# Pooled attention and two feed-forward blocks: in the first batch every second part of the attention weights meets the values in plain float32

## The chip, the cores and the metric

The program runs on one core of a Trainium2 chip. The metric is the device time of one execution, in microseconds (us); the number to compare with is the median of three runs of the kernel before, 1444.92 us (1443.05 to 1446.12). Engines: PE multiplies matrices (PEld is its weight load), ACT, DVE and POOL do elementwise work, SP issues most DMAs. PE's results go to PSUM, the tile `banks` of the program; the other tiles lie in SBUF.

## What is computed

```python
q_pool = q.reshape(B, H, S // 2, 2, D).mean(axis=3)            # B=4, H=8, S=1152, D=64
scores = (q_pool @ k.transpose(0, 1, 3, 2)) / np.sqrt(D)
attn = np.exp(scores - scores.max(-1, keepdims=True))
attn = attn / (attn.sum(-1, keepdims=True) + 1e-9)
x = attn @ v                                                   # then heads side by side: 2304 x 512
g = s * np.maximum(x @ w_in, 0.0) ** 2 + b                     # 512 -> 2048
x = g @ w_out                                                  # 2048 -> 512
out = (1 / (1 + np.exp(-(x @ w_gate)))) * (x @ w_val) @ w_out2 # 512 -> 1536 -> 512
```

All of it is float32. To keep float32's accuracy at a fast matmul, most operands are split in two: a rounded high part in the type `fp32r` and a low part, the rest.

## The kernel before, in words

**Planner.** The code does not issue instructions directly. Each step is added to a plan with a name, the engines that may do it, what it reads and writes and a rank; `Plan.order` then writes one order per engine, picking at each moment the ready step of the lowest rank for a free engine. A step with two engines goes to whichever is free first. A table, `MOVED`, shifts the rank and the place of every step by its name. Buffers are slots of a fixed number (`ROOM`); a slot's next tenant waits for the last one's readers. The order on every engine is therefore fixed in the program, and each engine runs its rows strictly in that order.

**Stages.** Attention goes batch by batch and in pairs of heads (`pair_prep` loads q, k and v of a pair and makes their transposed and split forms). Batch 0 is done by query rows (`pair_rows`), the other batches by key columns (`half_head_sums`). After a batch the first feed-forward block follows (`ffn1`) while the next batch's attention goes on beside it, and at the end the second block (`ffn2`) takes two batches at once. So the stretch up to about 191 us is batch 0's attention alone, with a few loads and splits of weights (the `w` steps) and a little of batch 1 in between.

**Batch 0's attention.** `block` multiplies the transposed q by k (L901), takes the row maximum on DVE (L908, L911) and the exponential with its sum on ACT (L915). `group(j, g, blocks, mid)` then turns the weights round: for one head `j` and a set of query blocks it goes over the 9 key chunks, two chunks at a time, or one at a time where the group also holds the middle block `mid`. Such a step is called a unit here. A unit's transposes (L946, and for the middle block a plain float32 matmul with the identity, L948) put 512 or 256 weights a partition into a bank (320 with the middle block). There are 4 head pairs, and in each pair two groups of 5 units and two of 9, so 28 units a pair and 112 in all.

From the bank a unit goes one of two ways, in turn (`unit[0] % 2`). On the *copy path* ACT copies the bank to an SBUF tile (`r p`, L469 `pp<-banks`), ACT or POOL makes the high part (`r p hi`, L462 or L464, `g<-pp`) and POOL or DVE the low part (`r p lo`, L472). On the *direct path* ACT rounds the bank into the high part (`r pT hi`, L469 `g<-banks`) and DVE subtracts it from the bank (`r pT lo`, L475). Either way PE then multiplies each chunk twice, high and low part, by the split values `vt` (L968, step `r pv`):

```python
for w in range(2):
    for i, c in enumerate(cs):
        nc.tensor.matmul(acc.t[:, :n], lhsT=vt[j].t[:, c, :2 * D], rhs=part(t, w)[:, i * n:(i + 1) * n],
                         start=(c == 0 and w == 0), stop=(c == NK - 1 and w == 1))
```

`vt` holds the low part of v in its first 64 columns and the high part in the next 64, so `acc` has two halves, which a copy and an addition put together at the group's end (`r o`, `r x add`). At a pair's end `x` is divided by the sums (L987 to L1004).

The values come by a load into one raw tile (`v load`, L683, `vn`, one slot), from which `v hi` and `v lo` make `vt` (two slots); the raw tile is free again as soon as `v lo` has read it.

Of the kernel before, what the change touches and what calls it, by code (L numbers as in the profile page):

```python
# [23 lines left out]

ROOM = dict(
    w=4, raw=3, xy=2, xx=1, r=2, g=4,
    qn=1, kn=1, vn=1, qT=2, kT=2, vt=2, st=6, pp=6,
    sg=2, mx=2, mc=2, r9=1, x=1, s=2, rs=1, rr=1,
    yy=1, yl=1, h=4, fo=9,
    ps=4, pr=8, pm=1, acc=5, ff=6, p2=3, wd=2, bank=8,  # L30
# [5 lines left out]


MOVED = {
    "q load": (-1, -9),
    "k load": (0, -100),  # L40
    "v load": (2.5, -102),
    "v hi": (0, 97),
    "v lo": (18, 38),
    "q add": (-3, 29),
    "q twice": (-2.5, -30),
    "pr qT": (-1.5, 69),
    "pr q hi False": (-6.5, 100),
    "pr q lo False": (-11, 68),
    "pr q hi True": (-6, 3),
    "pr q lo True": (45.5, -33),  # L50
    "pr kT": (-19.5, 79),
    "pr k hi": (-39.5, 10),
    "pr k lo": (-40, -29),
    "s b load": (-6.5, -46),
    "r qk 1": (-0.5, -351),
    "r max": (0, 32),
    "r - max": (-40, 11),
    "r exp": (40.5, -80),
    "r pT": (-32.5, 21),
    "r p": (-40, 84),  # L60
    "r p hi": (21.5, -68),
    "r p lo": (0, -21),
    "r pv": (-34, -88),
    "r pT hi": (-40, 101),
    "r pT lo": (8.5, 12),
    "r o": (0, 49),
    "r x add": (3, 116),
    "r qk 2": (-40, 112),
    "r sums": (60, 108),
    "r sums eps": (0, 33),  # L70
    "r 1 / sums": (-2, 2),
    "r spread": (8, -150),
    "r rows": (-0.5, -245),
    "r rows mid": (2, 74),
    "r x / sums": (55.5, -57),
    "r x / sums mid": (3, 63),
    "r end": (16, -111),
    "ps qT": (3, -59),
    "ps q hi False": (53, 89),
    "ps q lo False": (-27.5, -110),  # L80
    "ps kT": (-11, -1),
    "ps k hi": (11.5, -104),
    "ps k lo": (-37, 59),
    "xx hi": (59.5, -1),
    "xx lo": (60, 37),
    "w load": (-18, 34),
    "w top": (-19, 94),
    "w scale": (-13.5, -136),
    "w low": (-31, 18),
    "w join": (38.5, 14),  # L90
    "w sign": (-40, -93),
    "w hi": (-40, -95),
    "w lo": (-25.5, -32),
    "w keep": (0, -20),
    "one": (-33, -6),
    "ff xx up": (60, 125),
    "ff relu": (-11, -3),
    "square": (-40, 114),
    "g hi": (7, 20),
    "g lo": (-16, 108),  # L100
    "ff down": (55, -143),
    "ff y": (-11, 66),
    "column sum": (-7.5, 111),
    "ff y add": (31.5, 21),
    "bias": (-27, 149),
    "y bias": (-19, -30),
    "y store": (-25.5, 72),
    "qk": (0, 17),
    "s copy": (15.5, -5),
    "s max": (-14, 27),  # L110
    "max T": (-9.5, -130),
    "max": (46, -9),
    "max rows": (-27.5, -98),
    "s - max": (38.5, 169),
    "exp": (4, -43),
    "p hi": (-23, -97),
    "p lo": (-10.5, 18),
    "pv hi": (-40, 73),
    "pv lo": (18.5, -4),
    "sums": (36, -116),  # L120
    "x": (27.5, -8),
    "sums out": (6, -15),
    "sums in": (4, 112),
    "1 / sums spread": (0, -90),
    "1 / sums out": (0, -25),
    "1 / sums in": (3, 31),
    "x / sums": (26.5, -166),
    "1 / sums": (8, 22),
    "w fetch": (-3.5, -5),
    "w come": (59, -37),  # L130
    "x store": (42.5, -95),
    "turn": (42, -63),
    "yy load": (43.5, 45),
    "yy hi": (0, 79),
    "yy lo": (0, -86),
    "p2 yy up": (0, 47),
    "gate": (0, -40),
    "gate val": (-40, -79),
    "h hi": (19.5, -93),
    "h lo": (0.5, 95),  # L140
    "down 2": (-25.5, 139),
    "out": (60, 118),
    "out add": (-40, -64),
    "out store": (0, 82),
    "xx load": (42, -28),
    "p2 xx up": (-7, -54),
    "p2 relu": (13, 19),
    "p2 down": (0, -20),
    "p2 y": (19.5, -12),
    "p2 y add": (8, -91),  # L150
}


# [193 lines left out]
def kernel(  # L347
# [93 lines left out]
    def mm(n):  # L441
        return max(n / 2.4, 45) + 13.5
# [223 lines left out]
    def pair_prep(b, hp):  # L666
# [13 lines left out]
        for j in range(2):  # L680
            src = v[b, h0 + j].rearrange("(p c) d -> p c d", c=NK)
            vn = slot("ld", "vn", [P, NK, D])
            dma("v load", P * NK * D * 4, lambda vn=vn, src=src: nc.sync.dma_start(out=vn.t, in_=src), [], [vn], AT)  # L683
            t = plan.slot("vt", lambda k: vts[k])
            copy_sb("v hi", NK * D, lambda t=t: t.t[:, :, D:2 * D], lambda vn=vn: vn.t, [vn], [(t, 0)], AT)
            tt_sb("v lo", NK * D, lambda t=t: t.t[:, :, :D], lambda vn=vn: vn.t, lambda t=t: t.t[:, :, D:2 * D].bitcast(F32),
                  ALU.subtract, [vn, (t, 0)], [(t, 1)], AT)
            vt.append(t)

        def pairs_of_q():  # L690
# [188 lines left out]
    def pair_rows(hp, prep, x):  # L879
# [50 lines left out]
        unit = [0]  # L930

        def group(j, g, blocks, mid):

            n = 256 + (64 if mid else 0)
            acc = bank("acc")
            step = 1 if mid else 2
            for c0 in range(0, NK, step):
                cs = list(range(c0, min(NK, c0 + step)))
                ps = bank("pr")
                t = g_slot()  # L940
                m = n * len(cs)

                def issue(cs=cs, ps=ps):
# [19 lines left out]
                unit[0] += 1  # L963

                def pv(cs=cs, t=t):
                    for w in range(2):
# [180 lines left out]
```

## Time and profile before

| what | value |
| --- | --- |
| median of 3 runs | 1444.92 us (1443.05 to 1446.12) |
| the profiled execution: its time, its span | 1447.07 us, 1445.3 us |
| PE busy, weight load busy | 1380.4 us (96%), 1310.8 us (91%) |
| DVE, ACT, POOL busy | 1041.4 us (72%), 929.2 us (64%), 736.6 us (51%) |
| batch 0's attention | 0 to about 191 us |

The profiled execution took 2.15 us more than the median of the runs; 1.8 us of its time lies outside the span. "Busy" counts an instruction from start to end, and on PE the ends of one instruction overlap the start of the next. "Idle before" an instruction is time its engine waited, with the instruction that ended the wait behind the arrow. A wait costs time only where something that sets the end hangs on it.

### The profile page before, as it was taken

How to read it: one execution, taken by the hardware profiler on the slowest of the kernel's cores; microseconds unless marked ns; L12 is line 12 of the kernel's file. 1: busy time of each engine (PE TensorE's matmuls, PEld its weight loads, DVE VectorE, ACT ScalarE, POOL GpSimd, SP SyncE). 2: the span in 40 equal slices, each digit the busy share in tenths (PEclk: the TensorE clock that was granted, in tenths of full speed). 3: DMA queues.
4: the chain of work that ended last, by engine and by line, in shares of the span. 5: the costliest groups of instructions: out<-in, count | busy, mean ns of one | idle time of the engine just before them, and what ended most of it. 6: DMA issues, size and time to landing. Idle time of an engine off the chain costs nothing.

```text
span 1445.3 us, 25059 instructions
## 1 busy us (share of the span) xinstructions
PE 1380.4 (96%) x9164; PEld 1310.8 (91%) x9164; DVE 1041.4 (72%) x1786; ACT 929.2 (64%) x1987; POOL 736.6 (51%) x675
## 2 busy tenths in 40 slices
PE   6988998999999999999999999999999899999998
PEld 6867888888989999999899999999998899989897
DVE  6889897899989889889988757557473127737552
ACT  6889887988889898988899645333232434434130
POOL 3577675888867466666765446233232004325130
PEclk9999999999999999999999999999999999999999
DMA  3156123446435142413331463122137444313112
GB/s 91 50 166 202 26 92 100 153 152 222 143 108 167 50 142 79 137 47 115 106 133 47 178 256 126 59 88 88 59 92 247 165 154 147 116 58 118 42 61 66
DMA packets 103044, 167.89 MB, mean 116 GB/s; under 512 B 44652, under 2 KB 80264, under 8 KB 93832
## 3 DMA queue, kind: packets, MB, share of 16 engines
q1 hardware_dynamic: 96008, 115.95, 26.1%
q0 software_dynamic: 6912, 50.33, 9.8%
q8 instruction: 72, 1.18, 0.3%
q14 instruction: 52, 0.43, 0.1%
HBM read 139.99 MB, written 26.28 MB: 115 GB/s over the span
## 4 chain that ended last, share of the span: by engine, by line
PE 62%; ACT 13%; DVE 9%; DMA 7%; issue 5%; POOL 4%; SPq 0%; DVEq 0%; ACTq 0%; POOLq 0%
PE banks L540 13%; PE banks L542 13%; PE banks L541 13%; PE banks L770 3%; PE banks L1050 3%; PE banks L1049 3%; PE banks L1048 3%; ACT st L796 3%; ACT st L469 3%; DVE mx L475 3%; DMA raw<-in_moe_w_in_dram 2%; PE banks L818 2%; ACT pp L462 2%; PE banks L819 2%; PE banks L823 2%
## 5 line engine op out<-in xcount | busy, mean ns | idle before, releaser
L472 POOL TENSOR_TENSOR pp<-st,pp 128x864 fp32r<-128x864 f32 x94 | 199.3, 2130 | 32.3 <-ACT pp L462 29.7
L542 PE MATMUL banks<-yy,w 128*128 128x384 f32 x576 | 192.8, 335 | 0.0
L541 PE MATMUL banks<-yy,w 128*128 128x384 f32 x576 | 192.8, 335 | 0.0
L540 PE MATMUL banks<-yy,w 128*128 128x384 f32 x576 | 192.7, 335 | 0.0
L469 ACT COPY st<-banks 128x288 f32<-128x288 f32 x432 | 150.2, 409 | 41.2 <-PE banks L770 35.5
L475 DVE TENSOR_TENSOR mx<-banks,mx 128x288 f32<-128x288 f32 x336 | 151.3, 451 | 21.0 <-ACT st L469 10.5
L770 PE MATMUL banks<-qT,kT 128*128 128x288 f32 x864 | 162.3, 304 | 1.9 <-DVE mx L475 1.0
L540 PE MATMUL banks<-xx,w 128*128 128x288 f32 x512 | 155.1, 303 | 8.2 <-DMA w<-d_1u_1u 5.7
L541 PE MATMUL banks<-xx,w 128*128 128x288 f32 x512 | 151.7, 296 | 0.0
L475 DVE TENSOR_TENSOR st<-st,banks 128x864 f32<-128x864 f32 x144 | 149.4, 1041 | 3.1 <-PE banks L748 3.0
L542 PE MATMUL banks<-xx,w 128*128 128x288 f32 x512 | 151.6, 296 | 0.0
L540 PE MATMUL banks<-g,w 128*128 128x288 f32 x448 | 136.7, 305 | 3.7 <-ACT xy L642 2.9
L796 ACT ACTIVATE st<-st 128x864 f32<-128x864 f32 x144 | 132.9, 931 | 11.1 <-DVE st L475 10.1
L497 POOL TENSOR_SCALAR raw<-raw 128x512 f32<-128x512 f32 x98 | 66.5, 679 | 138.2 <-DMA raw<-in_moe_w_val_dram 50.5
L541 PE MATMUL banks<-g,w 128*128 128x288 f32 x448 | 133.7, 298 | 0.0
L542 PE MATMUL banks<-g,w 128*128 128x288 f32 x448 | 133.5, 298 | 0.0
L770 PEld LDWEIGHTS banks<-qT,kT 128*128 128x128 f32 x864 | 126.4, 188 | 5.9 <-DVE mx L475 3.8
L500 ACT ACTIVATE raw<-raw 128x512 f32<-128x512 f32 x104 | 70.7, 683 | 94.6 <-POOL raw L497 88.1
L818 PE MATMUL banks<-pp,vt 128*128 128x288 f32 x432 | 121.9, 302 | 7.6 <-ACT pp L462 5.8
L819 PE MATMUL banks<-pp,vt 128*64 128x288 f32 x432 | 118.5, 295 | 0.0
L540 PEld LDWEIGHTS banks<-yy,w 128*128 128x128 f32 x576 | 108.1, 188 | 0.3
L541 PEld LDWEIGHTS banks<-yy,w 128*128 128x128 f32 x576 | 108.1, 188 | 0.3
(145 smaller groups left out, 3867.3 us busy)
## 6 DMA issues: line engine op xcount, KB each, us to landing
w<-d_1u_1u POOLq DMA_DIRECT2D x24, 1024.0 KB, 5.6
w<-d_1d_1d POOLq DMA_DIRECT2D x24, 1024.0 KB, 5.8
raw<-in_moe_w_out_dram SPq DMA_DIRECT2D x40, 512.0 KB, 3.6
raw<-in_moe_w_gate_dram SPq DMA_DIRECT2D x24, 512.0 KB
raw<-in_moe_w_val_dram SPq DMA_DIRECT2D x24, 512.0 KB, 4.2
qn<-in_q_dram SPq DMA_DIRECT2D x16, 576.0 KB, 4.2
kn<-in_k_dram SPq DMA_DIRECT2D x32, 288.0 KB, 4.0
vn<-in_v_dram SPq DMA_DIRECT2D x32, 288.0 KB, 2.7
```

The costliest lines, as they stand in the source:

```text
L469: act(name, n, lambda: nc.scalar.copy(out=out(), in_=in_()), r, w, rank, sbuf=False)
L472: shared(name, n, lambda e: ENGINE[e].tensor_tensor(out=out(), in0=in0(), in1=in1(), op=op), r, w, rank, 2.15)
L475: dve(name, n, lambda: nc.vector.tensor_tensor(out=out(), in0=in0(), in1=in1(), op=op), r, w, rank)
L497: shared("w top", 512, lambda e: ENGINE[e].tensor_scalar(out=words(1).bitcast(F32), in0=words(1).bitcast(F32), scalar1=F64_TOP, scalar2=-F ...
L500: act("w scale", 512, lambda: nc.scalar.mul(words(1).bitcast(F32), words(1).bitcast(F32), 2.0 ** -112), [], [top], rank)
L540: nc.tensor.matmul(ps(), lhsT=whi(), rhs=xhi(), start=first, stop=False)
L541: nc.tensor.matmul((ps_lo or ps)(), lhsT=whi(), rhs=xlo(), start=False, stop=False)
L542: nc.tensor.matmul(ps(), lhsT=wlo(), rhs=xhi(), start=False, stop=last)
L770: nc.tensor.matmul(ps.t[:, :HQ], lhsT=kT.t[:, c], rhs=qq[:, w, hf * HQ:(hf + 1) * HQ], start=(w == 0), stop=(w == 1))
L796: act("exp", 3 * HQ, lambda s=s: nc.scalar.activation(out=s.t, in_=s.t, func=AF.Exp), [], parts, AT)
L818: nc.tensor.matmul(acc.t[:, :HQ], lhsT=vt.t[:, 3 * i + c, D:], rhs=hi.t[:, c], start=(i == c == 0), stop=False)
L819: nc.tensor.matmul(acc.t[:D, :HQ], lhsT=vt.t[:, 3 * i + c, :D], rhs=hi.t[:, c], start=False, stop=False)
```

## The change

In `group`, the flag `unit[0]` is gone and a flag `split` starts every group as true. A unit with `split` takes the copy path as before. The unit after it is taken whole: one copy of the bank to an SBUF tile in float32 (`r pT whole`, on ACT or DVE, whichever is free), no high and low part, and one matmul a chunk in plain float32 by the raw values (`r pv whole`, L972 in the changed file), added to the lower half of `acc`. Then `split` is true again. The direct path is gone. The raw values of a head must now stay until their last whole matmul, so `vn` has two slots. All ranks of `MOVED` are other numbers.

```diff
-    qn=1, kn=1, vn=1, qT=2, kT=2, vt=2, st=6, pp=6,
+    qn=1, kn=1, vn=2, qT=2, kT=2, vt=2, st=6, pp=6,
...
-    "r pT": (-32.5, 21),
+    "r pT": (-37.5, -107),
...
+            t.whole = vn
             vt.append(t)
...
+            split = True
             for c0 in range(0, NK, step):
...
-                t = g_slot()
+                t = g_slot() if split else slot("pp", "pp", [P, 3 * HQ])
...
-                if unit[0] % 2 == 0:
+                if split:
                     pc = slot("pp", "pp", [P, 3 * HQ])
...
                 else:
-                    copy_ps("r pT hi", m, lambda t=t, m=m: part(t, 0)[:, :m], lambda ps=ps, m=m: ps.t[:, :m], [ps], [(t, 0)], AT)
-                    tt_dve("r pT lo", m, lambda t=t, m=m: part(t, 1)[:, :m], lambda ps=ps, m=m: ps.t[:, :m],
-                           lambda t=t, m=m: part(t, 0)[:, :m].bitcast(F32), ALU.subtract, [ps, (t, 0)], [(t, 1)], AT)
-                unit[0] += 1
+                    def whole(e, ps=ps, t=t, m=m):
+                        if e == "ACT":
+                            nc.scalar.copy(out=t.t[:, :m], in_=ps.t[:, :m])
+                        else:
+                            nc.vector.tensor_copy(out=t.t[:, :m], in_=ps.t[:, :m])
+
+                    plan.add("r pT whole", {"ACT": 50 + 0.833 * m, "DVE": 70 + 1.04 * m}, 0, whole, [ps], [t], AT)
+                    v32 = vt[j].whole
+
+                    def pv32(cs=cs, t=t, v32=v32):
+                        for i, c in enumerate(cs):
+                            nc.tensor.matmul(acc.t[:D, :n], lhsT=v32.t[:, c], rhs=t.t[:, i * n:(i + 1) * n],
+                                             start=False, stop=False)
+
+                    pe("r pv whole", len(cs) * (n / 0.6 + 25), pv32, [t, v32], [acc], AT)
+                    split = True
+                    continue
...
+                split = False
```

Per pair this makes 16 split and 12 whole units out of 14 and 14. In all, 48 units are whole (16 of 512 and 32 of 320 elements) and 64 chunks go by a float32 matmul (32 of 256 and 32 of 320 columns); 160 fast matmuls stay in L968's place out of 288. The line numbers of the changed file are one higher from L687 on and up to fifteen higher below `group`.

The order moves in many places. Three carry the prediction. First PE, in the first pair's group with the middle block (`g` tiles are split units, `pp` tiles whole ones, `st` the weights that are turned, `vn` and `vt` the raw and the split values). Before:

```order
L901 MATMUL banks<-kT_198,qT_176 128x384 x4
L968 MATMUL banks<-g_384,vt_117 128x320 x2
L968 MATMUL banks<-g_388,vt_117 128x320 x2
L946 MATMUL banks<-ident,st_235 128x128
L946 MATMUL banks<-ident,st_268 128x128
L948 MATMUL banks<-ident,st_275 128x64
```

Now:

```order
L902 MATMUL banks<-kT_200,qT_176 128x384 x4
L947 MATMUL banks<-ident,st_340 128x128
L947 MATMUL banks<-ident,st_382 128x128
L949 MATMUL banks<-ident,st_276 128x64
L902 MATMUL banks<-kT_200,qT_176 128x384 x2
L972 MATMUL banks<-pp_410,vn_182 64x320
L982 MATMUL banks<-g_376,vt_117 128x320 x2
```

Two units gave four fast matmuls; two units now give one float32 matmul (64 output partitions) and two fast ones, and transposes for a later unit stand ahead of them.

Second DVE at the same place, first before and then now:

```order
L475 TENSOR_TENSOR xy_427<-pp_417 64x256
L475 TENSOR_TENSOR g_388<-banks,g_388 128x320
L475 TENSOR_TENSOR g_430<-banks,g_430 128x320
L908 TENSOR_REDUCE sg_224<-banks 128x1 x2
L911 TENSOR_REDUCE sg_224<-sg_224 128x1
L475 TENSOR_TENSOR g_458<-banks,g_458 128x320
```

```order
L475 TENSOR_TENSOR xy_401<-pp_393 64x256
L965 COPY pp_403<-banks 128x320
L965 COPY pp_410<-banks 128x320
L472 TENSOR_TENSOR g_372<-pp_407,g_372 128x320
L909 TENSOR_REDUCE sg_226<-banks 128x1 x3
L912 TENSOR_REDUCE sg_226<-sg_226 128x1
```

Subtractions that need ACT's high part have become copies that need the bank alone.

Third SP's queue, where the loads of the first two pairs stand, before and then now:

```order
L683 DMA vn_182<-in_v_dram 128x576
L673 DMA qn_194<-in_q_dram 128x1152
L677 DMA kn_220<-in_k_dram 128x9x64 x2
L683 DMA vn_255<-in_v_dram 128x576
L683 DMA vn_303<-in_v_dram 128x576
L677 DMA kn_561<-in_k_dram 128x9x64 x2
L683 DMA vn_597<-in_v_dram 128x576
L673 DMA qn_626<-in_q_dram 128x1152
```

```order
L683 DMA vn_182<-in_v_dram 128x576
L683 DMA vn_190<-in_v_dram 128x576
L673 DMA qn_196<-in_q_dram 128x1152
L677 DMA kn_222<-in_k_dram 128x9x64 x2
L677 DMA kn_521<-in_k_dram 128x9x64 x2
L683 DMA vn_566<-in_v_dram 128x576
L673 DMA qn_579<-in_q_dram 128x1152
L683 DMA vn_794<-in_v_dram 128x576
L492 DMA raw_870<-in_moe_w_in_dram 128x4x256
```

The first two value loads now come at once, and the second pair's (`vn_566`, `vn_794`) wait for the first pair's last whole matmuls, with a load of q and the first load of weights behind them.

## Rows read from the trace of the kernel before

**Rows 1.** The page's head.
```profile
span 1445.3 us, 25059 instructions
```

**Rows 2.** Busy time by stage: start and end, length, engines, clock, DMA share, GB/s.
```profile
0.00:191.00 191.00, 163.50 (x1113) 145.67 (x1114) 155.62 (x350) 159.13 (x458) 121.48 (x151) 0.99 0.36 106
191.00:850.00 659.00, 631.75 (x4652) 606.23 (x4652) 573.98 (x967) 565.67 (x1161) 441.87 (x340) 0.99 0.40 129
850.00:1445.30 595.30, 585.14 (x3403) 558.91 (x3401) 311.85 (x471) 204.41 (x368) 173.24 (x186) 0.99 0.33 106
```

**Rows 3.** Groups of instructions on PE, 0 to 191 us.
```profile
L968 PE MATMUL banks<-g,vt 128*128 128x320 f32 x144 | 31.5, 329 | 3.1 <-DVE kT L475 1.7 <-POOL g L472 1.0 <-DVE xy L475 0.3
L948 PE MATMUL banks<-ident,st 128*128 128x64 f32 x144 | 24.0, 249 | 0.0
L968 PE MATMUL banks<-g,vt 128*128 128x256 f32 x144 | 22.6, 289 | 1.6 <-ACT pp L469 0.8 <-ACT st L915 0.6 <-POOL g L472 0.2
```

**Rows 4.** PE in order of time: start, length, instructions.
```profile
25.50 2.13 PE L968 MATMUL banks<-g,vt 128*128 128x256 f32 x16
27.48 0.60 PE L946 MATMUL banks<-ident,st 128*128 128x128 f32 x4
...
36.84 0.82 PE L968 MATMUL banks<-g,vt 128*128 128x320 f32 x4
...
37.49 0.38 PE L946 MATMUL banks<-ident,st 128*128 128x128 f32 x2
...
37.71 0.33 PE L948 MATMUL banks<-ident,st 128*128 128x64 f32 x2
...
37.88 0.39 PE L946 MATMUL banks<-ident,st 128*128 128x128 f32 x2
```

**Rows 5.** Groups of instructions on ACT, 0 to 191 us.
```profile
L469 ACT COPY pp<-banks 128x320 f32<-128x320 f32 x44 | 17.9, 432 | 3.2 <-PE banks L948 1.6 <-PE banks L968 1.3
L469 ACT CAST g<-banks 128x320 fp32r<-128x320 f32 x36 | 15.6, 438 | 2.4 <-PE banks L948 2.3
L469 ACT CAST g<-banks 128x512 fp32r<-128x512 f32 x16 | 9.6, 610 | 1.5 <-PE banks L946 1.5
L462 ACT CAST g<-pp 128x320 fp32r<-128x320 f32 x13 | 5.8, 477 | 0.2
L469 ACT CAST g<-banks 128x256 fp32r<-128x256 f32 x4 | 1.6, 388 | 0.0
```

**Rows 6.** Groups of instructions on DVE, 0 to 191 us.
```profile
L475 DVE TENSOR_TENSOR g<-banks,g 128x320 fp32r<-128x320 f32 x36 | 17.5, 486 | 11.5 <-ACT g L469 11.3
L475 DVE TENSOR_TENSOR g<-banks,g 128x512 fp32r<-128x512 f32 x16 | 10.9, 684 | 1.2 <-ACT g L469 1.2
L472 DVE TENSOR_TENSOR g<-pp,g 128x320 fp32r<-128x320 f32 x5 | 2.8, 564 | 0.4 <-POOL g L464 0.4
L475 DVE TENSOR_TENSOR g<-banks,g 128x256 fp32r<-128x256 f32 x4 | 1.7, 417 | 0.1
```

**Rows 7.** Groups of instructions on POOL, 0 to 191 us.
```profile
L472 POOL TENSOR_TENSOR g<-pp,g 128x320 fp32r<-128x320 f32 x31 | 28.0, 910 | 5.1 <-ACT g L462 4.0
L472 POOL TENSOR_TENSOR g<-pp,g 128x512 fp32r<-128x512 f32 x15 | 19.4, 1301 | 2.6 <-ACT g L462 2.2
L472 POOL TENSOR_TENSOR g<-pp,g 128x256 fp32r<-128x256 f32 x4 | 2.9, 736 | 0.3
```

**Rows 8.** The chain of waits, 0 to 191 us, shares by line.
```profile
by line: PE banks L968 10.0%; DMA raw<-in_moe_w_in_dram 9.9%; PE banks L901 9.8%; PE banks L946 9.2%; issue 6.6%; DVE sg L908 6.6%; ACT st L915 6.1%; PE banks L948 3.3%; DMA raw<-in_moe_w_out_dram 3.0%; ACT pp L469 2.9%; PE banks L704 2.9%;
```

**Rows 9.** Waits, 0 to 191 us: total, times, longest.
```profile
ACT st L915 <- DVE sg L911: 7.4, 8, 1.6
DVE g L475 <- ACT g L469: 12.5, 16, 2.4
POOL vt L464 <- DMA vn<-in_v_dram: 9.9, 2, 7.2
SPq L683 <- POOL vt L472: 51.6, 6, 17.7
```

**Rows 10.** The raw values' tile: load to landing.
```profile
DMA to landing us min/median/max: 2.7/2.7/3.0
```

More of the change, by code (lines that the diff above doesn't have):

```diff
@@ L38 @@
 MOVED = {
[L39 to L56, printed above, removed]
@@ L57 @@
-    "r - max": (-40, 11),
-    "r exp": (40.5, -80),
-    "r pT": (-32.5, 21),
[L60 to L150, printed above, removed]
+    "q load": (-27, -111),
+    "k load": (0, 5),
+    "v load": (5, 0),
@@ new lines @@
+    "v hi": (-3.5, -18),
+    "v lo": (0, 109),
+    "q add": (0, -91),
+    "q twice": (-9.5, -70),
+    "pr qT": (0, 118),
+    "pr q hi False": (-1, -52),
+    "pr q lo False": (30, 59),
+    "pr q hi True": (0, -77),
+    "pr q lo True": (-10, -98),
+    "pr kT": (0, -69),
+    "pr k hi": (-30.5, 110),
+    "pr k lo": (-39.5, 31),
+    "s b load": (-22, -75),
+    "r qk 1": (4, -87),
+    "r max": (0, -31),
+    "r - max": (-40, -35),
+    "r exp": (45.5, 70),
+    "r pT": (-37.5, -107),
+    "r p": (-38.5, 128),
@@ new lines @@
+    "r p hi": (28, 65),
+    "r p lo": (-27, 49),
+    "r pv": (-40, 82),
+    "r pT whole": (0.5, -40),
+    "r pv whole": (19.5, 114),
+    "r o": (1.5, 83),
+    "r x add": (4.5, -84),
+    "r qk 2": (-40, 40),
+    "r sums": (10, -95),
+    "r sums eps": (-12.5, -11),
+    "r 1 / sums": (26.5, -34),
+    "r spread": (0, -17),
+    "r rows": (0, 13),
+    "r rows mid": (14, -107),
+    "r x / sums": (52, 92),
+    "r x / sums mid": (29, -17),
+    "r end": (-13, -36),
+    "ps qT": (57.5, -63),
@@ new lines @@
+    "ps q hi False": (24.5, -70),
+    "ps q lo False": (-16.5, 75),
+    "ps kT": (0, 52),
+    "ps k hi": (8, -100),
+    "ps k lo": (0, 30),
+    "xx hi": (13.5, 139),
+    "xx lo": (37.5, 144),
+    "w load": (0, -63),
+    "w top": (-28, 47),
+    "w scale": (0.5, 26),
+    "w low": (-34.5, -20),
+    "w join": (38.5, -117),
+    "w sign": (-30.5, 50),
+    "w hi": (-38, 40),
+    "w lo": (23, 15),
+    "w keep": (0, 60),
+    "one": (-10, 23),
+    "ff xx up": (60, 27),
+    "ff relu": (0, 83),
@@ new lines @@
+    "square": (-39, -96),
+    "g hi": (7.5, 48),
+    "g lo": (0, 64),
+    "ff down": (60, -92),
+    "ff y": (6.5, -44),
+    "column sum": (0, -108),
+    "ff y add": (13.5, 117),
+    "bias": (-11.5, -109),
+    "y bias": (0, -35),
+    "y store": (0, 29),
+    "qk": (19.5, 114),
+    "s copy": (1.5, 27),
+    "s max": (0, -71),
+    "max T": (16, 86),
+    "max": (60, 48),
+    "max rows": (6, 86),
+    "s - max": (38, 27),
+    "exp": (4.5, 16),
+    "p hi": (-31, 85),
+    "p lo": (-2, 56),
@@ new lines @@
+    "pv hi": (11, -110),
+    "pv lo": (56.5, -102),
+    "sums": (7.5, -109),
+    "x": (3, -92),
+    "sums out": (0, 29),
+    "sums in": (-2, 3),
+    "1 / sums spread": (23.5, 96),
+    "1 / sums out": (0, 38),
+    "1 / sums in": (0, -46),
+    "x / sums": (-23, 122),
+    "1 / sums": (0, 70),
+    "w fetch": (6.5, -108),
+    "w come": (22.5, 95),
+    "x store": (-39.5, -78),
+    "turn": (16.5, -9),
+    "yy load": (2, 87),
+    "yy hi": (60, 91),
+    "yy lo": (-20, 99),
+    "p2 yy up": (0, 37),
@@ L151 @@
+    "gate": (0, -32),
+    "gate val": (-31.5, -61),
+    "h hi": (13, -11),
+    "h lo": (32, -106),
+    "down 2": (-6.5, 29),
+    "out": (0, 165),
+    "out add": (-39, -114),
+    "out store": (0, 9),
+    "xx load": (0, 27),
+    "p2 xx up": (0, -89),
+    "p2 relu": (16, 41),
+    "p2 down": (0, 77),
+    "p2 y": (18, 10),
+    "p2 y add": (1, 96),
 }
@@ L928, in middle @@
             return block(MID, [(j, lambda w, j=j: qm[:, j, w], [("qm", j, w) for w in range(2)]) for j in range(2)])
-        unit = [0]
         def group(j, g, blocks, mid):
```

## The prediction

> **What bounds the kernel now.** I read the time by stages first. From 850 us on PE is busy 585.14 of 595.30 us while ACT has 204.41: there PE alone sets the pace. Between 191 and 850 us PE is busy 631.75 of 659.00 us, still the fullest engine. Up to 191 us, where all of the changed code runs, it is another matter: PE 163.50, ACT 159.13, DVE 155.62 and POOL 121.48 us of 191.00, nobody full [rows 2]. The clock that was granted is 0.99 in all three, so it plays no part. What follows batch 0's attention needs its result, so a microsecond that this stage loses or gains is carried to the end; the rest of the program has the same work before and after.
>
> In the first stage the reader should next look at who waits for whom. DVE's largest wait there is 12.5 us, in 16 waits, for ACT's rounding of a bank (the direct path), and ACT waits 7.4 us for DVE's maxima [rows 9]: the two hold each other up. The chain of waits through the stage changes engine all the time, with no line above 10.0% [rows 8]. So this is a stage of hand-overs between three or four engines that are each some 80% full; it shrinks if work and hand-overs go from the fullest of them, and grows if one of them is made the bound.
>
> How full PE really is decides the case. Its matmuls overlap: sixteen of 256 columns, of 289 ns each on average [rows 3], start within 1.98 us [rows 4]. So the busy 163.50 us overstates it, and I take the weight loads' 145.67 us as the fairer measure [rows 2]. By the one PE has 27.5 us of room in the stage, by the other 45.3; either holds the 17.2 us below, but PE would then be 95% full by the first and 85% by the second. The Trainium skill, Perfetto Trace Analysis, section Identifying the Most-Contended Engine, gives the same rule: matmul busy time misleads, weight loads tell more.
>
> **PE's part.** 64 chunks lose two fast matmuls each and get one float32 matmul. The price today: 16 fast ones of 256 columns take from 25.50 to the next start at 27.48 us, 0.124 us each; 4 of 320 columns from 36.84 to 37.49, 0.163 each [rows 4]. So a chunk costs 0.248 and 0.325 us. The float32 matmul with the identity is the nearest row for the new one: it is recorded 144 times for 72 matmuls, two records each [rows 3], and with 64 columns it lasts from 37.71 to 37.88, 0.17 us [rows 4]. Scaled by columns alone that gives 0.68 and 0.85 us, the upper bound; the lower bound is that its two records cost what two fast matmuls cost, nothing extra. Between them I go by the float32 transposes in front of it: two of 128 columns from 37.49 to 37.71, 0.11 us each or 0.86 ns a column [rows 4]. Two records at that rate make 1.72 ns a column, which leaves 0.06 us fixed of the 0.17. Then 256 columns cost 0.50 us and 320 cost 0.61, that is 0.252 and 0.285 more. **PE: 32 x 0.252 + 32 x 0.285 = +17.2 us**, with 0 and +30.6 us (32 x 0.43 + 32 x 0.525) as ends.
>
> **ACT's part.** The direct path's roundings go: 36 of 320, 16 of 512, 4 of 256 at 438, 610 and 388 ns [rows 5], 27.2 us. The changed order puts 19 of the 320-wide whole copies and 6 of the 512-wide ones on ACT, at 432 and (as the rounding of that size) 610 ns: +11.9. Eight more units are split (4 of 256, 4 of 320): copies at 388 and 432 ns, +3.3; and the order shows 9 more high parts on ACT at about 477 ns [rows 5], +4.3. **ACT: -7.7 us.**
>
> **DVE's part.** The subtractions from the bank go: 36 x 486 + 16 x 684 + 4 x 417 ns [rows 6], 30.1 us. The other whole copies come, 13 of 320 and 10 of 512; the trace has no such copy, and I charge the subtraction of the same size as its upper bound, +13.2 us (a copy reads one operand less, so a saving remains possible; ACT's 432 and 610 ns would make it 11.7). Ten more low parts are DVE's at 564 ns, +5.6. **DVE: -11.3 us**, and the 12.5 us of waiting for ACT's rounding go with the subtractions, for the copy waits for PE's transposes only.
>
> **POOL's part.** By the order it has three fewer low parts of 320, two fewer of 512, three more of 256, at 910, 1301 and 736 ns [rows 7]: **-3.1 us**. It has room in the stage, so this counts for nothing.
>
> **The values.** Their raw tile now lives until the last whole matmul of its head, so a second pair's load can only then start; it takes 2.7 us to land [rows 10]. Two slots and an early first load cover that as long as nobody needs the new tile within some 3 us. The pair's own order gives the first head half a pair (an eighth of the stage, some 24 us) and the second head the time of its neighbour's groups. I cost it at nothing; without the cover it is the third rival.
>
> **The sum.** If ACT, the fullest of the three elementwise engines, keeps its share of 159.13 in 191.00 us (83%), 7.7 us less of work makes the stage 9.2 us shorter. If PE comes to the same 83% with 145.67 + 17.2 = 162.9 us, the stage needs 195.5 us, 4.5 us more. These are the two ends of the mechanism. I take the middle of the gaining half, -4.5 us: the work of ACT, DVE and POOL falls by 22.1 us and a hand-over is gone from 48 units, while PE, at 85% by its loads, starts to hold others up. The other ranks move filling work about in the 191 to 850 us stage, where PE has 27 us of idle time in all [rows 2]; I cannot read a sign from the order and add 0, with some 4 us either way. The profiled execution (1447.07 us, span 1445.3 [rows 1]) would so become 1442.6, and since it stands 2.15 us above the median of the runs, the median becomes 1444.92 - 4.5 = about **1440.5 us**. Below, "the same" means within 0.2% (2.9 us), about what a measurement of this kernel can tell from no change.
>
> **Rivals.**
>
> *PE takes it back (the wash).* The sum over all four engines is -22.1 + 17.2, hardly anything, and the fullest engine is at 159 us before (ACT) and at 163 after (PE). For it speaks that PE has the largest shares of the stage's chain [rows 8]. Against it: the waits that go are real idle time on DVE. Time: 1442 to 1447.8.
>
> *PE becomes the bound (slower).* PE runs its rows in order, so a float32 matmul of 0.50 or 0.61 us stands in front of the q-by-k products and transposes for which ACT and DVE wait. L968 has 10.0% of the stage's chain, 19.1 us [rows 8], of 144 x 0.124 + 144 x 0.163 = 41.3 us of its work: 46% of it sets the pace. If the same share of the addition does, it costs 7.9 us, against some 3 us that the copies give back on the chain: +5, so 1450 us; with the upper price of the matmul (+30.6) it is +11. It decides once PE's additions exceed about 20 us, or once PE is truly 85% full where its rows stand.
>
> *The values come late.* SP's queue now holds a load of q and the first weight loads behind the second pair's values, which wait for PE. That queue already waits 51.6 us for a free values tile in six waits, and POOL once sat 7.2 us for one load [rows 9]. If one load a pair after the first is exposed by its 2.7 us, three pairs make +8 us: 1453.
>
> *The float32 matmul is no dearer than the pair.* Then PE's part is nothing and ACT's relief counts in full: -9, 1436 us. The Trainium skill, FP8 and Floating Point Precision, section TensorE Precision Notes, speaks against it with four passes for true float32; an estimate by that page (four times 0.124 and 0.163 us a chunk) would add 18.4 us in place of 17.2.
>
> **How the numbers follow.** The forecast (faster, about -4.5) 0.42; the wash 0.27; PE the bound 0.20; late values 0.06; the cheap matmul 0.05. So faster by over 0.2% is 0.47, the same 0.27, slower 0.26. The range goes down to 1432 (the stage's -9.2 with the ranks' 4) and up to 1451 (PE the bound); the likeliest case alone has 1435 to 1442.
>
> **What would show it.** Right: in the stage with batch 0's attention ACT's and DVE's busy time fall by about 8 and 11 us, DVE no longer waits for ACT's rounding, a float32 matmul takes 0.50 or 0.61 us until the next start, and batch 0's attention ends 4 to 5 us before 191 us; the later stages keep their lengths. Wrong: PE's idle time in the stage falls but its end does not move, or ACT's and DVE's waits for PE grow by as much as their work shrinks; or SP and POOL wait for values. A change of more than 4 us after batch 0 would be the ranks' doing and none of this working.

## The result, and the profile after

The changed kernel takes 1458.3 us (median of 3 runs, 1458.02 to 1458.88) against 1444.92 us (1443.05 to 1446.12): a ratio of 1.0098, 95% interval 1.0081 to 1.0114. It is 13.4 us **slower**. The forecast was 1440.5 us in a range up to 1451: wrong in sign, and outside the range.

The page's head, and the busy time by stage (columns as in [rows 2]; the first stretch is 9 us longer than there, since batch 0's attention now ends later):

```profile
span 1456.5 us, 25009 instructions
...
PE 1398.1 (96%) x9164; PEld 1308.4 (90%) x9164; DVE 1033.2 (71%) x1766; ACT 927.2 (64%) x1974; POOL 730.3 (50%) x668
```

```profile
0.00:200.00 200.00, 183.78 (x1108) 143.33 (x1109) 152.23 (x330) 157.04 (x449) 111.63 (x140) 0.98 0.35 103
200.00:850.00 650.00, 620.27 (x4601) 597.75 (x4600) 565.12 (x963) 559.53 (x1148) 440.19 (x336) 1.00 0.39 125
850.00:1456.50 606.50, 594.08 (x3459) 567.30 (x3457) 315.79 (x475) 210.63 (x379) 178.47 (x192) 0.99 0.34 109
```

In the first stretch PE went from 163.50 us of 191 [rows 2] to 183.78 of 200, though it loads fewer weights (143.33 us against 145.67). DVE, ACT and POOL are all less busy. Over the whole program DVE's busy time fell by 8.2 us, ACT's by 2.0 and POOL's by 6.3.

**Where the time went.** I take as a mark the first PE row behind batch 0's last product. PE in order of time there, before and then after (start, length, instructions):

```profile
187.13 0.86 PE L968 MATMUL banks<-g,vt 128*128 128x256 f32 x6
188.10 1.09 PE L770 MATMUL banks<-qT,kT 128*128 128x288 f32 x4
```

```profile
194.43 1.08 PE L972 MATMUL banks<-pp,vn 128*64 128x256 f32 x4
195.43 0.74 PE L982 MATMUL banks<-g,vt 128*128 128x256 f32 x4
196.11 1.08 PE L972 MATMUL banks<-pp,vn 128*64 128x256 f32 x4
197.12 0.50 PE L982 MATMUL banks<-g,vt 128*128 128x256 f32 x2
197.46 1.22 PE L771 MATMUL banks<-qT,kT 128*128 128x288 f32 x8
```

The mark moves from 188.10 to 197.46 us: +9.4. From there to the end it is 1257.2 us before and 1259.0 after: +1.8. These make the 11.2 us between the two profiled spans; the other 2.15 us is what the profiled execution of before stood above its median. So the loss is made in the stage that the change touches.

The waits up to 200 us (total, times, longest), the one row of before that the rows above lack, and then after:

```profile
DVE sg L908 <- PE banks L901: 5.2, 14, 1.4
```

```profile
ACT st L916 <- DVE sg L912: 19.6, 18, 2.4
PEld banks L982 <- issue: 17.9, 38, 1.3
DVE sg L909 <- PE banks L902: 17.0, 17, 2.5
...
PEld banks L972 <- issue: 6.8, 32, 0.3
```

DVE's 12.5 us of waiting for ACT's rounding [rows 9] are gone, as forecast. In their place DVE waits 17.0 us for PE's q-by-k products (5.2 before), and ACT, which needs DVE's maxima for its exponentials, 19.6 us (7.4 in [rows 9]). Together +24.0 us. The chain of waits says the same:

```profile
by line: PE banks L902 18.5%; PE banks L972 13.6%; PE banks L947 12.7%; PE banks L982 11.2%; issue 4.6%; PE banks L949 3.8%; PE banks L705 3.0%; DVE sg L909 3.0%; POOL g L472 2.7%; ACT st L916 2.6%; DMA raw<-in_moe_w_in_dram 2.4%; ACT pp L4
```

PE's lines named in it add up to 62.8%; those named in [rows 8] (L968, L901, L946, L948, L704) had 35.2%. The stage has gone from one that changes engine all the time to one that PE sets.

**What the new matmul costs.** PE and then the weight loads (PEld), both in order of time, in a group with the middle block; `[0.49 <-issue]` is idle time before the row, with no releaser that the profile shows:

```profile
38.53 0.75 PE L972 MATMUL banks<-pp,vn 128*64 128x320 f32 x2
39.22 0.56 PE L982 MATMUL banks<-g,vt 128*128 128x320 f32 x2
39.61 0.51 PE L902 MATMUL banks<-kT,qT 128*128 128x384 f32 x2
```

```profile
38.53 0.19 PEld L972 LDWEIGHTS banks<-pp,vn 128*64 128x64 f32 x2 [0.25 <-issue]
39.22 0.30 PEld L982 LDWEIGHTS banks<-g,vt 128*128 128x128 f32 x2 [0.49 <-issue]
```

A float32 chunk of 320 columns takes 0.69 us to the next start, and two of 256 take 1.00 to 1.01, so 0.50 each. But the fast pair behind it is dearer too: 0.39 us here for two of 320 columns, where before had 0.33, and 0.68 us for four of 256 columns (195.43 to 196.11), where before had 0.50, a quarter of the sixteen's 1.98 in [rows 4]. The second fence shows what goes with it: the weight loads of L972 and of the fast pair behind it start only when PE has come to them, after 0.25 and 0.49 us in which the loader does nothing. A whole and a split unit together now take 1.68 us for 256 columns (194.43 to 196.11; 0.99 before) and 1.08 for 320 (38.53 to 39.61; 0.65 before [rows 4]). If each of the 16 and 32 whole units pays that, PE's addition is 16 x 0.69 + 32 x 0.43 = **about 25 us**, of which the float32 matmuls alone, less the fast pairs in whose place they stand, make 19.7 (32 x 0.252 + 32 x 0.365); the forecast had 17.2.

### The profile page after: what moved, and what is told of

Same layout as the page of the kernel before. It is cut to its first block, busy times and chain, and to the rows that moved or that the text cites. A ratio compares the mean times of both kernels' runs of the same rounds, so it can differ in the third digit from the quotient of the medians.

```text
span 1456.5 us, 25009 instructions
## 1 busy us (share of the span) xinstructions
PE 1398.1 (96%) x9164; PEld 1308.4 (90%) x9164; DVE 1033.2 (71%) x1766; ACT 927.2 (64%) x1974; POOL 730.3 (50%) x668
## 4 chain that ended last, share of the span: by engine, by line
PE 60%; ACT 13%; DMA 9%; DVE 7%; POOL 5%; issue 5%; SPq 0%; DVEq 0%; POOLq 0%; ACTq 0%
PE banks L540 11%; PE banks L541 11%; PE banks L542 11%; PE banks L771 3%; ACT st L797 3%; PE banks L1064 3%; PE banks L1065 3%; PE banks L1063 3%; PE banks L902 3%; ACT st L469 3%; DVE mx L475 2%; ACT pp L462 2%; PE banks L972 2%; PE banks L947 2%; PE banks L824 2%
## 5 line engine op out<-in xcount | busy, mean ns | idle before, releaser
L469 ACT COPY st<-banks 128x288 f32<-128x288 f32 x432 | 153.1, 409 | 32.3 <-PE banks L771 26.4
L771 PE MATMUL banks<-qT,kT 128*128 128x288 f32 x864 | 158.9, 301 | 2.6 <-DVE mx L475 2.1
L797 ACT ACTIVATE st<-st 128x864 f32<-128x864 f32 x144 | 132.7, 934 | 10.6 <-DVE st L475 9.8
```

The lines of the kernel that those rows point to most:

```text
L469: act(name, n, lambda: nc.scalar.copy(out=out(), in_=in_()), r, w, rank, sbuf=False)
L771: nc.tensor.matmul(ps.t[:, :HQ], lhsT=kT.t[:, c], rhs=qq[:, w, hf * HQ:(hf + 1) * HQ], start=(w == 0), stop=(w == 1))
L797: act("exp", 3 * HQ, lambda s=s: nc.scalar.activation(out=s.t, in_=s.t, func=AF.Exp), [], parts, AT)
```

## The experiments

The theory at the start, **A**: PE's rows, run in order, are the bound, and the float32 matmul's price on PE is what is lost. **Rivals**: the other ranks are at fault (B); the values come late (C). What the relief of the other engines is worth beside it came in as a question of its own with run 5. In each run below the order of the rows on every engine is that of its base kernel but where the text says otherwise. The mark is the same as above; expectations that speak of the last product mean its own start, in before 187.7 us where the mark is at 188.10. Ratios are to the kernel before on the same chip.

A mark is read from one profile, and the profiles differ in the clock that PE was granted up to it: 1.00 in runs 2, 4, 8 and 9, 0.99 in before and run 7, 0.98 in after and runs 1, 3, 5 and 6, and 0.96 in run 10. A hundredth is 1.9 us of the stage, if all of it shows. So marks of after and of runs 1, 5 and 6 compare like with like, and the others carry a doubt of up to some 2 us for each hundredth.

**1. The whole unit by a fast matmul.** Base: after.

```diff
-                t = g_slot() if split else slot("pp", "pp", [P, 3 * HQ])
+                t = g_slot() if split else slot("pp", "pp", [P, 3 * HQ], F32R)
...
-    nc.tensor.matmul(acc.t[:D, :n], lhsT=v32.t[:, c], rhs=t.t[:, i * n:(i + 1) * n],
+    nc.tensor.matmul(acc.t[:D, :n], lhsT=vt[j].t[:, c, D:2 * D], rhs=t.t[:, i * n:(i + 1) * n],
```

> The changed kernel with the same order on every engine, but the whole units' matmul takes the rounded values and weights of type fp32r (one fast matmul of 64 output partitions a chunk), so their low parts are left out of the result. Theory A (PE's price: the float32 matmuls pace batch 0's attention): a chunk falls from 0.50 or 0.68 us to about 0.15, some 28 us less work on PE in the stage, and the time goes back by 8 us or more, to 1444-1450 us. Theory B (the other ranks make worse orders): 1455-1459, for the order is the same. Theory C (the values held until the last whole matmul come late for the next pair): 1444-1450 too, since the raw values are not read by PE here; the next kernel tells A from C.

Measured: 1449.33 us, ratio 1.0033 (1.0018 to 1.0047). The mark, on PE in order of time:

```profile
186.12 1.09 PE L771 MATMUL banks<-qT,kT 128*128 128x288 f32 x7
```

With the matmul's price gone, the stage ends 11.3 us earlier than after, and even 2.0 us earlier than before, with some 9 us less PE work than before (one matmul a chunk in place of two). The price of the float32 matmul is the loss in the stage, and rival B falls as a cause of it: the ranks and the order here are those of after.

**2. The values freed early.** Base: after; the float32 matmul reads the high part of `vt`, bits as they stand, so that `vn` is free as early as before.

```diff
-    nc.tensor.matmul(acc.t[:D, :n], lhsT=v32.t[:, c], rhs=t.t[:, i * n:(i + 1) * n],
+    nc.tensor.matmul(acc.t[:D, :n], lhsT=vt[j].t[:, c, D:2 * D].bitcast(F32), rhs=t.t[:, i * n:(i + 1) * n],
```

> The changed kernel, same order, float32 matmuls as they are, but with the high part of the values read as float32 in place of the raw values (their low part is left out for the whole units), so the raw tile is free once it is split. Theory C: 1444-1450 us, and SP no longer waits for the whole matmuls with its value loads (59 us in three waits in the changed kernel). Theories A and B: 1456-1460, no difference that can be measured.

Measured: 1456.29 us, ratio 1.0085 (1.0066 to 1.0103). SP's queue no longer waits for L972; of after it had this row:

```profile
SPq L683 <- PE banks L972: 59.2, 3, 21.4
```

Here it is gone, and the stage ends where it did (PE in order of time):

```profile
197.67 1.22 PE L771 MATMUL banks<-qT,kT 128*128 128x288 f32 x8
```

The queue's 59 us of waiting cost nothing that shows at the stage's end. The rival of late values falls.

**3 and 4. Ranks and structure apart.** Run 3: after with the ranks of before (the whole unit's two steps take the ranks of `r pT hi` and `r pv`). Run 4: before with the ranks of after. Here the order moves everywhere. The first lines of run 3's edit (run 4 is the other way round):

```diff
-    "r pT": (-37.5, -107),
+    "r pT": (-32.5, 21),
...
```

> The changed kernel with the table of ranks of the kernel before (the whole copy takes the rank of the direct path's rounding, the whole matmul that of the fast one). Theory B: 1444-1450 us. Theory A: batch 0's attention ends at 195 us or later, PE as full as in the changed kernel, 1455-1470 (the old ranks are not made for it).

> The kernel before with the changed table of ranks (the direct path's rounding takes the whole copy's rank, its subtraction keeps its own). Theory B: 1455 us or more, with batch 0's attention no later than 192 us if B acts after it. Theory A: within 1440-1452, and batch 0's attention ends at about 188-192 us.

Measured: 1513.15 us, ratio 1.0479 (1.0457 to 1.05), and 1473.31 us, ratio 1.0207 (1.0185 to 1.023). PE at the mark, in run 3 and then in run 4:

```profile
218.10 0.95 PE L771 MATMUL banks<-qT,kT 128*128 128x288 f32 x6
```

```profile
187.05 0.53 PE L783 MATMUL banks<-ident,mx 128*96 128x128 f32 x3
```

The new ranks alone do not lengthen the stage (187.05, where before has 188.10), but what follows takes 1284.8 us in place of 1257.2 (span 1471.8). With the old ranks the new structure loses in both parts (span 1511.8). Run 4 came out as theory B forecast and against A, run 3 lies above both. What the two show is that each table of ranks does better with the structure that it came with: the change's own table takes 20.6 us out of the stage that the old one would give. Neither crossing can be read as "the ranks' share" of the change. What the changed order costs in the stage is read from runs 1 and 5, which keep it and end the stage no later than before.

**5. Only the matmul put back.** Base: after; two fast matmuls a chunk in place of the float32 one, on 128 weight columns as before. PE's work is that of before, while ACT, DVE and POOL keep the relief.

```diff
-    nc.tensor.matmul(acc.t[:D, :n], lhsT=v32.t[:, c], rhs=t.t[:, i * n:(i + 1) * n],
-                     start=False, stop=False)
+    for w in range(2):
+        nc.tensor.matmul(acc.t[:, :n], lhsT=vt[j].t[:, c, :2 * D], rhs=t.t[:, i * n:(i + 1) * n],
+                         start=False, stop=False)
```

> The changed kernel, same order, but each chunk of a whole unit goes by two fast matmuls of 128 output partitions as in the kernel before (the rounded weights, counted twice, without their low part), so PE has the kernel before's work and no float32 matmul, while ACT's, DVE's and POOL's relief stays. It measures that relief alone. Theory A1 (the relief is worth the 4.5 us that I forecast, PE's price ate it): the last product of batch 0 ends at about 183 us and the time is 1439-1442. Theory A2 (the relief is worth next to nothing, since the stage hangs on hand-overs and not on how full ACT and DVE are): the last product at 186-189 us, 1444-1450.

Measured: 1447.77 us, ratio 1.0023 (1.001 to 1.0037). PE to the mark, the waits, and the chain by line:

```profile
185.92 0.64 PE L973 MATMUL banks<-pp,vt 128*128 128x256 f32 x4
186.40 0.69 PE L983 MATMUL banks<-g,vt 128*128 128x256 f32 x4
186.92 0.64 PE L973 MATMUL banks<-pp,vt 128*128 128x256 f32 x4
187.40 0.78 PE L983 MATMUL banks<-g,vt 128*128 128x256 f32 x2
188.01 1.22 PE L771 MATMUL banks<-qT,kT 128*128 128x288 f32 x8
```

```profile
ACT st L916 <- DVE sg L912: 15.9, 17, 3.0
...
DVE sg L909 <- PE banks L902: 10.6, 13, 2.0
```

```profile
by line: PE banks L902 13.0%; PE banks L947 11.5%; issue 6.8%; DVE sg L909 5.8%; DMA raw<-in_moe_w_in_dram 5.5%; ACT kT L469 5.3%; ACT st L916 5.3%; PE banks L983 4.9%; PE banks L949 3.3%; PE banks L973 3.3%; ACT pp L469 2.7%; PE banks L705
```

This is the run that decides. ACT, DVE and POOL are 5.0, 6.4 and 7.6 us less busy than before over the program, yet the mark is at 188.01 us, where before has 188.10: **the relief of ACT, DVE and POOL, in the order that came with it, gains 0.1 us in this stage**, or up to some 2 us if the lower clock here (0.98 against 0.99) hid a part. What it would be worth in another order was not tried. DVE and ACT wait more instead: 10.6 us for the products (5.2 before) and 15.9 us for the maxima (7.4 [rows 9]). And a whole and a split unit take 1.00 us (185.92 to 186.92) where after took 1.68: that difference is all that sets the two kernels apart on PE, and at the same clock the mark lies 9.45 us earlier.

**6. Only the addition on PE, in the kernel before.** The direct path's fast matmuls go out twice: 72 chunks, two more each, 36 x 2 x 0.163 + 36 x 2 x 0.124 = 20.7 us [rows 4]. Nothing else changes. (`unit[0]` is counted up just ahead of the first line.)

```diff
+    direct = unit[0] % 2 == 0
...
-    nc.tensor.matmul(acc.t[:, :n], lhsT=vt[j].t[:, c, :2 * D], rhs=part(t, w)[:, i * n:(i + 1) * n],
-                     start=(c == 0 and w == 0), stop=(c == NK - 1 and w == 1))
+    for again in range(2 if direct else 1):
+        nc.tensor.matmul(acc.t[:, :n], lhsT=vt[j].t[:, c, :2 * D], rhs=part(t, w)[:, i * n:(i + 1) * n],
+                         start=(c == 0 and w == 0 and again == 0),
+                         stop=(c == NK - 1 and w == 1 and again == (1 if direct else 0)))
```

> The kernel before, same order, with every fast matmul of the direct units issued twice (the result counts them twice): 72 chunks x 2 x about 0.145 us, some 21 us more work on PE in batch 0's attention and nothing else changed, about what the change adds. Theory A: the stage grows by 7-11 us and the time is 1451-1456. Theory D (PE's added work is hidden in its idle time and it is the changed order or the copies that cost): no more than 3 us, 1445-1448.

Measured: 1456.11 us, ratio 1.008 (1.0067 to 1.0094). PE at the mark, and the chain by line:

```profile
200.09 0.69 PE L770 MATMUL banks<-qT,kT 128*128 128x288 f32 x4
```

```profile
by line: PE banks L971 25.4%; PE banks L901 16.1%; PE banks L946 12.0%; PE banks L948 4.7%; PE banks L704 4.3%; issue 3.5%; ACT st L915 3.2%; ACT pp L469 2.8%; DVE sg L908 2.7%; DMA raw<-in_moe_w_out_dram 2.7%; DVE g L475 1.9%; DMA qn<-in_q
```

The stage is 12.0 us longer, 58% of what was added (some 10 us, 50%, if the clock's 0.98 against 0.99 made up the rest), and both it and the time lie a little above theory A's ranges. PE's lines have 62.5% of the chain: the picture of the changed kernel (62.8%), made from the kernel before by PE work alone.

**7. The float32 matmul twice.** Base: after.

```diff
-    nc.tensor.matmul(acc.t[:D, :n], lhsT=v32.t[:, c], rhs=t.t[:, i * n:(i + 1) * n],
-                     start=False, stop=False)
+    for w in range(2):
+        nc.tensor.matmul(acc.t[:D, :n], lhsT=v32.t[:, c], rhs=t.t[:, i * n:(i + 1) * n],
+                         start=False, stop=False)
```

> The changed kernel, same order, with every float32 matmul issued twice in a row (the whole units count twice): 64 more, 32 of 256 and 32 of 320 columns. If PE paces the stage already, most of their work shows: by the records of 0.25 and 0.34 us some 38 us of work, 20-35 us more time, 1480-1495. If the stage hangs on hand-overs: 5-12 us, 1463-1472. Its trace also gives the price of a float32 matmul that follows another, apart from the change between the two kinds: 0.50 and 0.68 us again if the price is all in the columns, less if part of it is paid once a unit.

Measured: 1485.05 us, ratio 1.0275 (1.026 to 1.0291). PE in order of time:

```profile
30.59 1.94 PE L973 MATMUL banks<-pp,vn 128*64 128x256 f32 x8
32.47 0.51 PE L983 MATMUL banks<-g,vt 128*128 128x256 f32 x2
...
37.31 1.29 PE L973 MATMUL banks<-pp,vn 128*64 128x320 f32 x4
38.53 0.56 PE L983 MATMUL banks<-g,vt 128*128 128x320 f32 x2
...
224.99 1.22 PE L771 MATMUL banks<-qT,kT 128*128 128x288 f32 x8
```

Four float32 matmuls of 256 columns take 1.88 us where two took 1.01, so a further one costs 0.435; two of 320 take 1.22 where one took 0.69, so 0.53. The first of a unit costs more than a further one, by 1.01 - 0.87 = 0.14 and 0.69 - 0.53 = 0.16 us: that is paid once a unit, however many follow. The Trainium skill, FP8 and Floating Point Precision, section TensorE Precision Notes, gives float32 four passes; four of the fast matmuls would be 0.50 and 0.65 us, so a further one stays somewhat under that, and the first one, at 0.575 and 0.69, somewhat above. The addition is 32 x 0.435 + 32 x 0.53 = 30.9 us, and the mark moves from 197.46 to 224.99: 27.5 us, 89% of it.

**8 and 9. A saving on PE that was none.** The middle block's float32 matmul with the identity (0.17 us) becomes a transpose of the 64 rows that are wanted, in before (8) and in after (9).

```diff
-    nc.tensor.matmul(ps.t[:, i * n + 256:i * n + 320], lhsT=mid.t[:, c * P:(c + 1) * P],
-                     rhs=ident[:, j * 64:(j + 1) * 64], start=True, stop=True)
+    js64 = slice(j * 64, (j + 1) * 64)
+    nc.tensor.transpose(ps.t[:, i * n + 256:i * n + 320], mid.t[js64, c * P:(c + 1) * P],
+                        ident[js64, js64])
```

> The kernel before, same order on every engine; the float32 matmul of the middle block with a part of the identity (72 of them, two records, 0.17 us each) becomes a transpose of the 64 rows that are wanted (one record of 64 columns). PE loses some 72 x 0.10 = 7 us in batch 0's attention and nothing else changes. If PE's work in this stage is exposed at the 59% that doubling the direct units' matmuls showed: 4 us less, 1439-1442 us, the last product of batch 0 at 183-185 us. If what is taken from PE is worth as little as what was taken from ACT and DVE: within 1.5 us of the kernel before.

> The changed kernel, same order, with the same replacement for the middle block: 7 us less work on PE. If PE paces the stage more fully here (its added float32 matmuls made it the bound), more of it shows than in the kernel before: 5-7 us, 1450-1453 us, the last product of batch 0 at 190-192 us in place of 197. If not: 1456-1458.

Measured: 1450.55 us, ratio 1.0044 (1.0026 to 1.0061), and 1468.43 us, ratio 1.0173 (1.0146 to 1.0199): slower, both against the expectation. In run 8, PE and then the weight loads in order of time, and the wait by its total:

```profile
31.88 0.44 PE L946 MATMUL banks<-ident,st 128*128 128x128 f32 x2 [0.46 <-ACT pp L469]
32.25 0.27 PE L949 MATMUL banks<-ident,st 64*128 64x64 f32 x1
32.45 0.44 PE L946 MATMUL banks<-ident,st 128*128 128x128 f32 x2
```

```profile
32.25 0.14 PEld L949 LDWEIGHTS banks<-ident,st 64*128 64x128 f32 x1 [0.17 <-issue]
```

```profile
PEld banks L949 <- issue: 12.1, 72, 0.2
```

Two transposes and the middle one take 0.57 us (31.88 to 32.45) where they took 0.39 (37.49 to 37.88 [rows 4]): the load of 64 rows stands 0.17 us idle first, 72 times. The saving was a cost of 72 x 0.18 = 13 us, and so the run is one more addition to PE: the mark moves by 4.5 us in before (192.57) and by 8.5 us in after (205.91). PE at the mark, in run 8 and then in run 9:

```profile
192.57 0.53 PE L770 MATMUL banks<-qT,kT 128*128 128x288 f32 x2
...
205.91 1.22 PE L771 MATMUL banks<-qT,kT 128*128 128x288 f32 x8
```

Up to the mark both runs had a clock of 1.00, where before had 0.99 and after 0.98, so the cost can be up to 2 us more in run 8 and up to 4 in run 9.

**10. The same saving without the 64-row load.** Base: before; the middle block is turned with all its 128 rows, ahead of the bank's two other transposes, which overwrite the half that isn't wanted. The rows are those of before but for this.

```diff
+    if mid:
+        nc.tensor.transpose(ps.t[:, 256 - j * 64:384 - j * 64], mid.t[:, c * P:(c + 1) * P], ident)
     for k, bl in enumerate(blocks):
         nc.tensor.transpose(ps.t[:, i * n + k * P:i * n + (k + 1) * P], bl.t[:, c * P:(c + 1) * P], ident)
-    if mid:
-        nc.tensor.matmul(ps.t[:, i * n + 256:i * n + 320], lhsT=mid.t[:, c * P:(c + 1) * P],
-                         rhs=ident[:, j * 64:(j + 1) * 64], start=True, stop=True)
```

> The kernel before, with the middle block's float32 matmul by 64 columns of the identity (72 of them, two records each, 0.17 us) replaced by a full transpose of its 128 columns (one record, 0.11 us, weight load of all 128 rows), issued ahead of the two other transposes of its bank, which overwrite the half that is not wanted. Nothing else moves. PE gets about 72 x 0.06 = 4 us less to do in batch 0's stage. Theory A (PE's rows are on the stage's path, 40 to 60 % of any difference shows): the stage's last product is issued 1.5 to 3 us earlier than at 187.7 us, and the time is 1442 to 1443.5 against 1444.5. Rival (the order is tuned to the old durations, so that any deviation, shorter too, makes waits of its own): the last product comes no earlier, and the time is the same or up to 3 us longer.

Measured: 1444.91 us (1441.94 to 1449.71), ratio 1.0002 (0.9989 to 1.0015): no difference. On PE the three now take 0.32 us, with the mark at 190.13:

```profile
36.10 0.27 PE L946 MATMUL banks<-ident,st 128*128 128x128 f32 x1
36.21 0.38 PE L948 MATMUL banks<-ident,st 128*128 128x128 f32 x2
36.42 0.27 PE L946 MATMUL banks<-ident,st 128*128 128x128 f32 x1
...
190.13 1.10 PE L770 MATMUL banks<-qT,kT 128*128 128x288 f32 x4
```

PE has 72 x 0.07 = 5 us less to do and the stage isn't shorter; in this one profile it is 2.0 us longer, at a granted clock of 0.96 up to 190 us where before has 0.99 [rows 2], so this mark can't be read to 2 us. The times show nothing of theory A's 1.5 to 3 us, and their interval leaves at most 1.6 of it; whether the rival (an order that fits the old durations) is right, or the clock hid the gain, isn't settled. What a saving on PE is worth can be read between runs 5 and 1, which had the same order and the same clock up to the mark: 128 fast matmuls become 64, some 9.2 us less, and the mark comes 1.9 us earlier (188.01 to 186.12), 21%. No version here beats the kernel before.

## Why the prediction was wrong

**What held.** The place: 9.4 of the 11.2 us between the spans are batch 0's attention, and the rest of the program moved by 1.8 us, within the "0, with some 4 us either way" that the ranks were given. DVE's wait for ACT's rounding went. The values cost nothing (run 2). The price of the float32 matmul itself, 0.50 and 0.61 us, was near: 0.50 and 0.69.

**The step that failed is the sum**: "If ACT ... keeps its share of 159.13 in 191.00 us (83%), 7.7 us less of work makes the stage 9.2 us shorter", and then the choice of "the middle of the gaining half". Run 5 gives ACT, DVE and POOL their relief with PE as before, and the stage ends at 188.01 against 188.10 us: that end of the mechanism is -0.1, at most some -2 with the clock allowed for, and not -9.2. ACT, 83% busy in this stage of hand-overs, was not a bound that shrinks with its work; ACT and DVE waited longer for one another and for PE's products instead. The same paragraph's other end, PE at +4.5, was the right sign, and half the size.

**The second step that failed** was PE's room: "I take the weight loads' 145.67 us as the fairer measure", hence 85% full with the addition. It leaned on the Trainium skill, Perfetto Trace Analysis, section Identifying the Most-Contended Engine, which judges PE's headroom by weight loads and by the share of peak. Here the measurement decides otherwise: run 6 adds 20.7 us to those 145.67 of 191, which by that measure still fit, and 12.0 of them show at the stage's end. Of the 45.3 us in which the loader of before stood idle, 30.5 were waits for ACT (15.8) and DVE (14.7); the reading that fits run 6 is that a row put in front delays what these wait for in turn; that is argued, not shown row by row. By the marks as they stand, 34% (4.5 of 13 us, run 8), 38% (9.4 of 25, the change itself) and 58% (run 6) of an addition come out at the end from the kernel before's level; on top of the change it is 65% (8.5 of 13, run 9) and 89% (run 7). The clock's part makes each of these uncertain by up to 2 us of the numerator, in run 9 by up to 4; the order, less than 60% from before and more on top of the change, stands with it.

**A term was mis-sized**: PE's +17.2 us measured about 25. The 320-column matmul was 0.69 in place of 0.61, and the forecast priced the new matmul alone: the weight load that did not go ahead, of the float32 matmul and of the fast pair behind it, was no term. ACT's -7.7 us held for the rows that it priced (its own first term is 27.1, not 27.2): by count and mean length 27.1 us of roundings went, and 15.6 of copies and 3.9 of high parts came, -7.6. DVE's rows came to -7.0 in place of -11.3, since the low parts that it took over cost 9.9 us and not 5.6 (those of 320 took 782 ns each, not 564). By run 5 neither matters.

**The rival that was right** is "PE becomes the bound": its point of decision, "once PE's additions exceed about 20 us", was passed. It reckoned 46% of 17.2 us less 3 us that the copies give back; with 25 us and nothing given back, its own 46% makes 11.5 us, where 9.4 were measured. It had a chance of 0.20, since it was set beside a gain on ACT and DVE that the chain of before hardly shows: in [rows 8] ACT and DVE stand with L915 and L908, which the change leaves alone, and with the copy path's L469; the direct path's rounding and subtraction are not among the lines named. Among the pieces of that chain they have some 6 us of 191, such as these two, and run 5 did not gain even that:

```profile
67.51 0.39 ACT g L469
67.92 0.49 DVE g L475
```

**Open.** Runs 1 and 5 are 0.2 to 0.3% slower than before though their stage ends no later: 5.3 and 3.0 us. The executions of one kernel spread over some 9 us (before: 1439.53 to 1448.75 in the set of run 10), and their granted clock goes with the time: over the four sets, the executions of before at a clock of 0.997 have a median of 1442.8 us, those at 0.991 of 1447.8. So the prediction's "it plays no part", read from 0.99 in all three stages, is too strong for differences of a few us. The twelve executions of run 1 had a mean clock of 0.9914, those of before beside them 0.9946; an estimate of what that costs is 0.0032 of 1445 us, up to 4.6 of the 5.3 us. For run 5 (0.9930 against 0.9941) it is up to 1.6 of the 3.0. Why the clock was lower in these executions isn't shown.

## What to carry to other kernels

Before work is moved from elementwise engines to PE, issue some of PE's instructions twice and look at how much of it reaches the end of the stage: at run 6's 58% the forecast's own 17.2 us cost 10, more than the 9.2 us that it hoped to gain at best, and no share of busy time said so. Do not count the relief of an engine as time before its rows are seen on the chain of waits; here they had 6 us of it and gave 0.1. And an instruction's price includes what it does to its neighbours: measure from the start of the unit to the start of what follows it, a change of matmul kind and back included.

## What was not expected of the hardware

- The weights of a float32 matmul between `fp32r` matmuls, and of the fast pair behind it, were not loaded ahead: 0.25 us idle before the one, 0.49 before the other (6.8 us in 32 waits and 17.9 in 38). A second float32 matmul in the same unit costs 0.435 or 0.53 us, the first some 0.15 more.
- A transpose of 64 rows between transposes of 128 waited 0.17 us for its weight load each time, and so cost more than a float32 matmul of 64 columns by full rows (0.57 against 0.39 us for the three).
- The granted clock from 16 to 24 us was 1.00 in before and 0.79 in after and in run 5, and the same twelve products (from 18.6 us) took 3.7 us there where they took 2.35. From 19 to 21 us of after the granted clock was 0.50, the lower of its two levels (1.2 and 2.4 GHz). In all three PE had stood idle 1.9 us up to 17.4 us, so the rows do not show what made the difference. It is no part of the 9.45 us between run 5 and after, which both have it; of the 9.4 between before and after it can be up to 2.
